# Retention and a gated linear unit on one core: units of 256 tokens with two tokens per partition, and attention products in 64x64 tiles of TensorE

## The chip, the core and the metric

The kernel runs on one core of a Trainium2 chip. The core has TensorE (matmuls, results to PSUM), VectorE, ScalarE and GpSimd (elementwise work), SyncE (here it only issues transfers) and 16 DMA engines. In the profile they are PE (and PEld for its weight loads), DVE, ACT, POOL and SP. The time is the device time of one execution in microseconds; a kernel's time is the median over its runs.

## The reference

There are 8 batches of 576 tokens, 8 heads of width 64. Each head has a decay `gamma = 1 - 2^(-5-h)`. The first part is causal attention without a softmax, weighted by `gamma` to the power of the distance; the second a gated linear unit, whose gate is a causal convolution of five taps per channel:

```python
scores = (1/8) * q @ k.T                               # per batch and head, 576 x 576
ret    = scores * where(i >= j, gamma ** (i - j), 0)
x      = (ret @ v)            # heads side by side: (8, 576, 512)
gate   = sigmoid(sum over t of conv_w[t] * x[:, i - 4 + t, :])
out    = (gate * (x @ w_val)) @ w_out                  # float32, (8, 576, 512)
```

`gamma ** (i - j)` is a product of a factor for `i` and one for `j`. The kernel puts the latter into `v` (tile `gin`) and the former, with the 1/8, onto the result (tile `gout`), so that a mask of ones and zeros is all that a block of scores needs, and what earlier tokens give can be carried in a 64x64 state per head, the sum of `k` times scaled `v`. Inputs and output are float32; the matmuls are bfloat16.

## The kernel before

A chunk is 128 tokens of one batch, one token per partition, all heads. A batch has four full chunks; the last 64 tokens of two batches make a tail chunk. The chunks go through in two groups of four batches, 36 in all. Two neighbouring chunks are a unit of the second part, 256 tokens, 18 in all (a unit of the tails holds 64 tokens of four batches).

For a chunk: `load` issues three transfers on SP's queue, whose runs in memory are one head's row of one token, 256 bytes (L77, L84). `cast` makes bfloat16 copies of k and q and scales v, on GpSimd (L191 to L193). `turn` transposes k and q on TensorE, a pair of heads at a time, into a PSUM tile that VectorE copies for k and ScalarE for q (L205 to L209). `scores` multiplies them in two half-height tiles (64 rows, 128 columns) of TensorE into two PSUM banks (L220); `masks` multiplies each bank by the mask on VectorE (L229). `carried` adds the state's part for a pair of heads with a full 128x128 matmul, the state's off-diagonal blocks being zero (L244, L250). `values` multiplies the masked scores with v in two half-width tiles (L261), and `take_x` scales the result into `xg`, channels on partitions (L270, L274). `update` accumulates the state in a PSUM bank over the chunks of a batch (L289), and ScalarE copies the two diagonal blocks out (L300).

For a unit: `conv` multiplies `xg`, shifted by the tap, with diagonal 64x64 matrices, four tiles of TensorE at once (L322). `gate` is ScalarE's sigmoid (L330). `value` is the product with `w_val` (L337), multiplied by the gate on VectorE (L340); `project` is the product with `w_out` (L347), which ScalarE copies from PSUM (L350) and SP stores, 128 tokens to a transfer (L353, L356).

The order on every engine is written out by hand in the last loop, one slot per chunk (L362 to L401). In slot t the loads of chunk t+6 are issued and chunk t+4 is cast; scores and masks are those of t+1, values and update those of t, transposes those of t+2. A unit's convolution, gate and values stand in the even slots, its projections in the odd ones. PSUM has eight banks: one for transposes, two for scores, one for the attention result, one for the state, three shared by convolution, values and projection.

Of the kernel before, what the change touches and what calls it, by code (L numbers as in the profile page):

```python
# [13 lines left out]
F32 = mybir.dt.float32  # L14
# [7 lines left out]
def kernel(  # L22
# [14 lines left out]
    P = 128  # L37
# [5 lines left out]
    LA = 8  # L43
# [5 lines left out]
    half = ctx.enter_context(tc.tile_pool(name="half", bufs=2))  # L49
    bfp = ctx.enter_context(tc.tile_pool(name="bfp", bufs=4))  # L50
    tp_sb = ctx.enter_context(tc.tile_pool(name="tsb", bufs=3))
    pp = ctx.enter_context(tc.tile_pool(name="pp", bufs=2))
    gp = ctx.enter_context(tc.tile_pool(name="gp", bufs=2))
    op_sb = ctx.enter_context(tc.tile_pool(name="osb", bufs=3))
    xp = ctx.enter_context(tc.tile_pool(name="xp", bufs=1))
    ps_t = ctx.enter_context(tc.tile_pool(name="pst", bufs=1, space=PSUM))
    ps_s = ctx.enter_context(tc.tile_pool(name="pss", bufs=1, space=PSUM))
    ps_o = ctx.enter_context(tc.tile_pool(name="pso", bufs=1, space=PSUM))
    ps_st = ctx.enter_context(tc.tile_pool(name="psst", bufs=1, space=PSUM))
    ps_g = ctx.enter_context(tc.tile_pool(name="psg", bufs=3, space=PSUM))  # L60


    chunks = []
    for g in range(B // GB):
        for b in range(g * GB, (g + 1) * GB):
            chunks += [("full", b, c) for c in range(NCH)]
        chunks += [("tail", b, NCH) for b in range(g * GB, (g + 1) * GB, 2)]
    NT = len(chunks)

    with tc.manual_schedule():  # L70

        loaded = {}

        def load_chunk(b, c):
            for name, src in (("k", k), ("q", q), ("v", v)):
                t = half.tile([P, H, D], F32, name=f"f{name}c", bufs=LA + 1)
                nc.sync.dma_start(out=t, in_=src[b, :, c * P:(c + 1) * P, :].rearrange("h p d -> p h d"))  # L77
                loaded[name, "full", b, c] = t

        def load_tail(b):  # L80
            for name, src in (("k", k), ("q", q), ("v", v)):
                t = half.tile([P, H, D], F32, name=f"f{name}c", bufs=LA + 1)
                for i in range(2):
                    nc.sync.dma_start(out=t[i * TAIL:(i + 1) * TAIL],  # L84
                                      in_=src[b + i, :, NCH * P:S, :].rearrange("h p d -> p h d"))
                loaded[name, "tail", b, NCH] = t

        def load(t):
            kind, b, c = chunks[t]
            if kind == "full":  # L90
                load_chunk(b, c)
            else:
                load_tail(b)

        load(0)
        load(1)

# [4 lines left out]
        nc.scalar.dma_start(out=wvf, in_=moe_w_val.rearrange("(o i) n -> i o n", i=P))  # L102
        load(2)
        wo_src = moe_w_out.rearrange("(pr ab hl p) n -> ab hl p pr n", pr=2, ab=2, hl=2)
        for (p0, blk, ab, hl) in ((0, 0, 0, 0), (64, 0, 1, 0), (0, 2, 1, 1), (64, 2, 0, 1)):
            nc.scalar.dma_start(out=wof[p0:p0 + 64, blk:blk + 2, :], in_=wo_src[ab, hl])
        for t in range(3, LA - 2):
            load(t)
# [7 lines left out]
        nc.vector.tensor_copy(identf, ident[0:32, 0:32])  # L116

        mask = consts.tile([P, P], BF16, name="mask")
        nc.gpsimd.memset(mask, 1.0)
        nc.gpsimd.affine_select(mask, mask, pattern=[[1, P]], base=0, channel_multiplier=-1,  # L120
                                compare_op=ALU.is_ge, fill=0.0)
        mask_t = consts.tile([P, P], BF16, name="maskt")
        nc.vector.tensor_copy(mask_t, mask)
        nc.vector.memset(mask_t[0:64, 64:128], 0.0)

        lrow = consts.tile([P, H], F32, name="lrow")
        lcol = consts.tile([P, NP], F32, name="lcol")
        for h in range(H):
            nc.vector.memset(lrow[:, h:h + 1], -lng[h])
            nc.vector.memset(lcol[(h % 2) * 64:(h % 2) * 64 + 64, h // 2:h // 2 + 1], lng[h])  # L130
        toki = consts.tile([P, NCH + 1], mybir.dt.int32, name="toki")
        nc.gpsimd.iota(toki, pattern=[[P, NCH + 1]], base=0, channel_multiplier=1)
        tok = consts.tile([P, NCH + 1], F32, name="tok")
        nc.vector.tensor_copy(tok, toki)
        nc.vector.tensor_scalar(tok[64:128, NCH:NCH + 1], tok[64:128, NCH:NCH + 1], -64.0, None, op0=ALU.add)
        gin = consts.tile([P, NCH + 1, H], F32, name="gin")
        nc.vector.tensor_tensor(gin, tok.unsqueeze(2).to_broadcast([P, NCH + 1, H]),
                                lrow.unsqueeze(1).to_broadcast([P, NCH + 1, H]), op=ALU.mult)
        nc.scalar.activation(gin, gin, AF.Exp)

        posi = consts.tile([P, S], mybir.dt.int32, name="posi")
        nc.gpsimd.iota(posi, pattern=[[1, S]], base=0, channel_multiplier=0)
# [7 lines left out]
        sbd = [consts.tile([P, NP, P], BF16, name=f"sbd{i}") for i in range(2)]  # L150
        sbl = [consts.tile([P, NP, P], BF16, name=f"sbl{i}") for i in range(GB)]
        for t in sbd + sbl:
            nc.gpsimd.memset(t, 0.0)
# [8 lines left out]
        def prep_conv():  # L162
            cps = ps_t.tile([P, KC * NP], F32, name="tps")
# [10 lines left out]
        def prep_wv():  # L174

            src = wvf.rearrange("p o (pr ab hl j) -> p o pr ab hl j", pr=2, ab=2, hl=2)
            for (blk, j0, ab, hl) in ((0, 0, 0, 0), (0, 64, 1, 0), (2, 0, 1, 1), (2, 64, 0, 1)):
                nc.scalar.copy(wvb[:, :, blk:blk + 2, j0:j0 + 64], src[:, :, :, ab, hl, :])
# [3 lines left out]


        bf = {}

        def cast(t):
            kind, b, c = chunks[t]
            kb = bfp.tile([P, H, D], BF16, name="kb")
            qb = bfp.tile([P, H, D], BF16, name="qb")
            vb = bfp.tile([P, H, D], BF16, name="vb")  # L190
            nc.gpsimd.tensor_copy(kb, loaded["k", kind, b, c])  # L191
            nc.gpsimd.tensor_copy(qb, loaded["q", kind, b, c])  # L192
            nc.gpsimd.tensor_tensor(vb, loaded["v", kind, b, c],  # L193
                                    gin[:, c, :].unsqueeze(2).to_broadcast([P, H, D]), op=ALU.mult)
            bf[t] = (kb, qb, vb)

        tsb = {}

        def turn(t):
            kb, qb, vb = bf[t]  # L200
            ps = ps_t.tile([P, 2, NP, P], BF16, name="tps")
            for i, src in enumerate((kb, qb)):
                flat = src.rearrange("p h d -> p (h d)")
                for pr in range(NP):
                    nc.tensor.transpose(ps[:, i, pr, :], flat[:, pr * P:(pr + 1) * P], ident)  # L205
            kt = tp_sb.tile([P, NP, P], BF16, name="kt")
            qt = tp_sb.tile([P, NP, P], BF16, name="qt")
            nc.vector.tensor_copy(kt, ps[:, 0])  # L208
            nc.scalar.copy(qt, ps[:, 1])  # L209
            tsb[t] = (kt, qt)  # L210

        sps = {}

        def scores(t):
            kt, qt = tsb[t]
            s = [ps_s.tile([P, NP, P], F32, name=f"s{i}") for i in range(2)]
            for pr in range(NP):
                for i in range(2):
                    r = slice(i * 64, i * 64 + 64)
                    nc.tensor.matmul(s[i][:, pr, :], lhsT=kt[r, pr, :], rhs=qt[r, pr, :],  # L220
                                     start=(pr == 0), stop=(pr == NP - 1), skip_group_check=True)
            sps[t] = s

        pt = {}

        def masks(t, i):
            m = mask if chunks[t][0] == "full" else mask_t
            p = pp.tile([P, NP, P], BF16, name=f"p{i}")
            nc.vector.tensor_tensor(p, sps[t][i], m.unsqueeze(1).to_broadcast([P, NP, P]), op=ALU.mult)  # L229
            pt[t, i] = p  # L230

        ops = {}
        state = {}

        def carried(t):

            kind, b, c = chunks[t]
            o = ps_o.tile([P, NP, P], F32, name="o")
            ops[t] = o
            qt = tsb[t][1]  # L240
            if kind == "full":
                if c:
                    for pr in range(NP):
                        nc.tensor.matmul(o[:, pr, :], lhsT=state[b][:, pr, :], rhs=qt[:, pr, :],  # L244
                                         start=(pr == 0), stop=False, skip_group_check=True)
            else:
                for pr in range(NP):
                    for i in range(2):
                        cs = slice(i * TAIL, (i + 1) * TAIL)
                        nc.tensor.matmul(o[:, pr, cs], lhsT=state[b + i][:, pr, :], rhs=qt[:, pr, cs],  # L250
                                         start=(pr == 0 and i == 0), stop=False, skip_group_check=True)

        def values(t):
# [25 lines left out]
        def update(t):  # L279
# [4 lines left out]
            if c == 0:  # L284
                st[b] = ps_st.tile([P, NP, P], F32, name="st")
# [145 lines left out]
```

## Time and profile before

| what | value |
|---|---|
| median of 3 runs | 195.38 us (195.11 to 197.34) |
| span of the profiled execution, first to last instruction | 194.1 us |
| median less the profiled span | 1.3 us |
| granted TensorE clock, mean over the span | 0.986 of full speed |
| TensorE matmul busy, weight loads | 152.2 us in 2273, 111.0 us in 2273 |
| VectorE, ScalarE, GpSimd busy | 114.3, 89.3, 86.9 us |
| moved by DMA | 40.21 MB in 118919 packets, 113242 of them under 512 bytes |
| SP's queue (inputs and outputs) | 117760 packets, 37.76 MB, 86.3% of 16 engines' time |
| inputs, 256 KB each: issue to landing | 4.8 to 5.3 us |
| outputs, 256 KB each: issue to landing | 3.8 us |

An execution's own time is given for the timed runs alone; for the profiled one the page has its span, and sums are made against that. Busy time is the union of an engine's instructions. A matmul's duration there is its latency, so the rate of a series is read from its starts. The slices are fortieths of the span, 4.85 us each, with busy shares in tenths. The chain of waits goes back from the last instruction, at each step to what released it. A line of the groups has the source line, engine, operation, output and inputs, shapes and count, then busy time, mean duration in ns, and the idle time before these instructions with what ended it.

### The profile page before, as it was taken

To read this page: it belongs to the slowest core of one execution; us is meant where nothing else is said; L and a number is where in the kernel's file an instruction comes from. 1 tells how busy PE (TensorE), PEld (TensorE's weight loads), DVE (VectorE), ACT (ScalarE), POOL (GpSimd) and SP (SyncE) were. 2 spreads that over 40 slices of the span, in tenths; PEclk is the share of its full clock that TensorE was granted. 3 is DMA by queue.
4 is the path that set the end of the run, shared out by engine and by line. 5 is a ranking of instruction groups with operands and counts; after the bars stand their busy time and mean duration, and the time that the engine had idled before them with its cause. 6 is when DMAs were issued, how large, how long until landed. Compare 5 with 4: busy or idle time off the path is not lost.

```text
span 194.1 us, 5639 instructions
## 1 busy us (share of the span) xinstructions
PE 152.2 (78%) x2273; PEld 111.0 (57%) x2273; DVE 114.3 (59%) x211; ACT 89.3 (46%) x183; POOL 86.9 (45%) x126
## 2 busy tenths in 40 slices
PE   0112666998898989898988899788989898979990
PEld 0001545775666676667766576666666666667740
DVE  6406774747475657575766657474766575747420
ACT  0072635354646454444435464446463535354431
POOL 8214685655454626453644534454445362520000
PEclk9999999699999999999999999999999999999997
DMA  5999999999999999799999795999997998931124
GB/s 136 287 205 163 220 223 182 234 221 200 256 250 238 247 230 255 158 243 216 277 193 281 169 282 127 231 231 280 233 237 187 245 253 187 237 142 62 52 105 108
DMA packets 118919, 40.21 MB, mean 207 GB/s; under 512 B 113242, under 2 KB 113262, under 8 KB 118894
## 3 DMA queue, kind: packets, MB, share of 16 engines
q1 hardware_dynamic: 117760, 37.76, 86.3%
q10 hardware_dynamic: 1134, 2.11, 4.2%
q8 instruction: 17, 0.28, 0.7%
q14 instruction: 8, 0.07, 0.1%
HBM read 30.42 MB, written 9.44 MB: 205 GB/s over the span
## 4 chain that ended last, share of the span: by engine, by line
PE 48%; DMA 18%; ACT 12%; DVE 9%; SPq 4%; issue 4%; POOL 1%; ACTq 0%; DVEq 0%; POOLq 0%
PE g L337 10%; PE g L347 9%; PE g L322 9%; DMA fvc<-in_v_dram 7%; ACT qt L209 6%; DMA out_dram<-ob 5%; DMA fkc<-in_k_dram 5%; PE tps L205 5%; PE s L220 5%; PE o L261 4%; ACT gate L330 4%; PE st L289 4%; DVE kt L208 4%; DVE p L229 3%; SPq L77 2%
## 5 line engine op out<-in xcount | busy, mean ns | idle before, releaser
L229 DVE TENSOR_TENSOR p<-s,mask 128x512 bf16<-128x512 f32 x64 | 43.7, 684 | 19.3 <-PE s L220 19.3
L337 PE MATMUL g<-xg,wvb 128*128 128x256 bf16 x288 | 37.1, 272 | 14.7 <-ACT gate L330 13.4
L193 POOL TENSOR_TENSOR vb<-fvc,gin 128x512 bf16<-128x512 f32 x36 | 37.5, 1043 | 22.2 <-DMA fvc<-in_v_dram 16.0
L340 DVE TENSOR_TENSOR z<-gate,g 128x512 bf16<-128x512 f32 x36 | 24.8, 688 | 33.4 <-ACT gate L330 24.7
L337 PEld LDWEIGHTS <-wvb 128*128 128x128 bf16 x288 | 27.3, 97 | 21.1 <-issue 18.3
L191 POOL CAST kb<-fkc 128x512 bf16<-128x512 f32 x36 | 22.9, 636 | 31.9 <-DMA fkc<-in_k_dram 21.1
L192 POOL CAST qb<-fqc 128x512 bf16<-128x512 f32 x36 | 22.2, 617 | 29.4 <-DMA fqc<-in_q_dram 29.2
L347 PE MATMUL g<-wob,z 128*128 128x512 bf16 x144 | 34.4, 380 | 0.3 <-DVE z L340 0.3
L209 ACT COPY qt<-tps 128x512 bf16<-128x512 bf16 x36 | 21.1, 585 | 26.8 <-DVE kt L208 25.6
L350 ACT COPY ob<-g 128x512 f32<-128x512 f32 x36 | 21.0, 589 | 19.7 <-DMA out_dram<-ob 14.1
L300 ACT CAST sbd<-st 64x256 bf16<-64x256 f32 x48 | 17.6, 367 | 25.2 <-PE st L289 24.7
L322 PE MATMUL g<-xg,dg 64*64 64x256 bf16 x720 | 23.2, 271 | 0.0
L208 DVE COPY kt<-tps 128x512 bf16<-128x512 bf16 x36 | 15.1, 421 | 11.8 <-PE tps L205 11.7
L270 DVE TENSOR_TENSOR xg<-o,gout 128x512 bf16<-128x512 f32 x32 | 21.8, 681 | 0.0
L347 PEld LDWEIGHTS <-z 128*128 128x128 bf16 x144 | 13.3, 99 | 13.7 <-DVE z L340 1.2
L205 PE MATMUL tps<-ident,kb 128*128 128x128 bf16 x144 | 14.9, 229 | 7.1 <-POOL kb L191 7.1
L330 ACT ACTIVATE gate<-g 128x512 f32<-128x512 f32 x36 | 19.6, 601 | 1.7 <-PE g L322 1.7
L322 PEld LDWEIGHTS <-dg 64*64 64x64 bf16 x720 | 18.4, 106 | 2.0 <-issue 0.4
L205 PE MATMUL tps<-ident,qb 128*128 128x128 bf16 x144 | 14.9, 229 | 5.7 <-POOL qb L192 5.7
L220 PE MATMUL s<-qt,kt 64*128 64x128 bf16 x288 | 15.0, 225 | 4.5 <-ACT qt L209 4.3
L220 PEld LDWEIGHTS <-kt 64*128 64x128 bf16 x288 | 10.1, 96 | 10.2 <-DVE kt L208 4.1
L261 PE MATMUL o<-p,vb 128*64 128x128 bf16 x288 | 15.4, 230 | 0.0
(45 smaller groups left out, 108.1 us busy)
## 6 DMA issues: line engine op xcount, KB each, us to landing
fkc<-in_k_dram SPq DMA_DIRECT2D x32, 256.0 KB, 5.0
fqc<-in_q_dram SPq DMA_DIRECT2D x32, 256.0 KB, 5.3
fvc<-in_v_dram SPq DMA_DIRECT2D x32, 256.0 KB, 4.8
out_dram<-ob SPq DMA_DIRECT2D x32, 256.0 KB, 3.8
wvf<-in_moe_w_val_dram ACTq DMA_DIRECT2D x1, 1024.0 KB, 9.7
wof<-in_moe_w_out_dram ACTq DMA_DIRECT2D x4, 256.0 KB, 10.5
fkc<-in_k_dram SPq DMA_DIRECT2D x8, 128.0 KB, 3.4
fqc<-in_q_dram SPq DMA_DIRECT2D x8, 128.0 KB, 3.3
```

Source lines behind the costliest of these rows:

```text
L191: nc.gpsimd.tensor_copy(kb, loaded["k", kind, b, c])
L193: nc.gpsimd.tensor_tensor(vb, loaded["v", kind, b, c], gin[:, c, :].unsqueeze(2).to_broadcast([P, H, D]), op=ALU.mult)
L205: nc.tensor.transpose(ps[:, i, pr, :], flat[:, pr * P:(pr + 1) * P], ident)
L209: nc.scalar.copy(qt, ps[:, 1])
L220: nc.tensor.matmul(s[i][:, pr, :], lhsT=kt[r, pr, :], rhs=qt[r, pr, :], start=(pr == 0), stop=(pr == NP - 1), skip_group_check=True)
L229: nc.vector.tensor_tensor(p, sps[t][i], m.unsqueeze(1).to_broadcast([P, NP, P]), op=ALU.mult)
L261: nc.tensor.matmul(o[r, pr, :], lhsT=vb[:, 2 * pr + i, :], rhs=pt[t, i][:, pr, :], start=(fresh and pr == 0), stop=(pr == NP - 1), skip_gr ...
L322: nc.tensor.matmul(g[bank][cols, pr, :], lhsT=dg[rows, blk, kk, :], rhs=xs(n, rows, blk, kk), start=(pr == 0 and kk == 0), stop=(pr == 1 a ...
L330: nc.scalar.activation(t, gps[n][i], AF.Sigmoid)
L337: nc.tensor.matmul(vps[:, j, :], lhsT=wvb[:, o, 2 * i + j, :], rhs=xs(n, slice(0, P), o, PAD), start=(j == 0 and o == 0), stop=(j == 1 and ...
L340: nc.vector.tensor_tensor(z, gsb[n][i], vps, op=ALU.mult)
L347: nc.tensor.matmul(o, lhsT=zsb[n, j // 2][:, j % 2, i * P:(i + 1) * P], rhs=wob[:, j, :], start=(j == 0), stop=(j == NP - 1))
```

## The change

The kernel is rewritten around units of 256 tokens; both parts go unit by unit.

- A partition holds two neighbouring tokens, so a run of the inputs is 512 bytes and of the output 4 KB. A tail unit has four batches' last 64 tokens, 32 partitions each. Loads are issued four units ahead, and a unit's output is one tile and one transfer (four for a tail), issued in the next unit's step behind that step's loads.
- The two tokens of a partition are index `r`. Tokens stand in PSUM in the order (r, a), token 2a + r of 128; masks and `gout` follow it, and `take_x` writes them back in order.
- All attention products are 64x64 tiles of TensorE, issued in rounds of four (`QUAD`), one for each quarter of the array: transposes (64 a unit), scores (32), masked products (32), update (32). The carried state uses the two tiles that lie on one diagonal and then those on the other.
- Masks and the PSUM copies of transposes take two banks in one instruction. ScalarE now copies k and q; the state is summed on GpSimd from a float32 copy that ScalarE makes.
- PSUM: two banks shared by transposes and convolution, two by scores and update, two for the attention result, two for values and projections. All four of the first kinds have a single buffer.
- The value and output weights are loaded on SP's queue between inputs. Eight products of zeros are issued at the start. In the first unit GpSimd casts units 0 and 1 before the first state sums, k of unit 0 is cast on VectorE, and two small copies (`fence`) part the first carried products.

```diff
-        def load_chunk(b, c):
...
+        def load1(n, u):
+            t = ldp.tile([P, H, 2 * D], F32, name=f"f{n}c")
+            if kind == "full":
+                nc.sync.dma_start(out=t, in_=src[b, :, c * W:(c + 1) * W, :].rearrange("h (p r) d -> p h (r d)", r=2))
...
-        nc.scalar.dma_start(out=wvf, in_=moe_w_val.rearrange("(o i) n -> i o n", i=P))
-        load(2)
+        nc.sync.dma_start(out=wvf, in_=moe_w_val.rearrange("(o i) n -> i o n", i=P))
+        load(1)
...
+    QUAD = ((0, 0), (1, 1), (0, 1), (1, 0))
...
+        def turn(u):
+            ps = ps_a.tile([P, 2, 2, 2, 2, 2, 64], BF16, name="a")
+            for hf in range(2):
+                for i in range(2):
+                    for prl in range(2):
+                        for r in range(2):
+                            for (c, par) in QUAD:
+                                h = 2 * (2 * hf + prl) + par
+                                nc.tensor.transpose(ps[half[par], c, hf, i, prl, r, :], bf[u][i][half[c], h, r, :],
+                                                    ident[half[c], half[c]])
...
+        def take_turn(u, hf):
+            nc.scalar.copy(kqt[u][hf].rearrange("p c i l r a -> p c (i l r a)"),
+                           tps[u][:, :, hf].rearrange("p c i l r a -> p c (i l r a)"))
...
+        def scores(u, hf, between=None):
+            s = ps_s.tile([P, 2, 2, 2, P], F32, name="s")
+            t = kqt[u][hf]
+            for prl in range(2):
+                for r in range(2):
+                    for (c, par) in QUAD:
+                        nc.tensor.matmul(s[half[c], par, prl, r, :], lhsT=t[half[par], c, 0, prl, r, :],
+                                         rhs=t[half[par], c, 1, prl, :, :].rearrange("p r a -> p (r a)"),
+                                         start=True, stop=True, skip_group_check=True)
+                    if between and prl == 0 and r == 0:
+                        between()
...
+        def masks(u, hf):
+            nc.vector.tensor_tensor(p.rearrange("p e l r a -> p (e l) (r a)"),
+                                    sps[u, hf].rearrange("p e l r a -> p (e l) (r a)"),
+                                    m.rearrange("p r a -> p (r a)").unsqueeze(1).to_broadcast([P, 4, W]), op=ALU.mult)
...
+        def carried(u, odd):
+            for pr in range(NP):
+                t = kqt[u][pr // 2]
+                for c in range(2):
+                    par = c ^ odd
+                    rows = half[par]
...
+                        nc.tensor.matmul(o[rows, c, pr, :], lhsT=st[rows, pr, :],
+                                         rhs=t[rows, c, 1, pr % 2, :, :].rearrange("p r a -> p (r a)"),
...
+        def values(u, hf):
+            for prl in range(2):
+                for r in range(2):
+                    for (c, par) in QUAD:
+                        nc.tensor.matmul(o[half[par], c, pr, :], lhsT=vb[half[c], 2 * pr + par, r, :],
+                                         rhs=p[half[c], par, prl, r, :], start=first(u, c, par),
...
+        def update(u):
+            xy = ps_s.tile([P, 2, 512], F32, name="s")
+            for pr in range(NP):
+                for r in range(2):
+                    for (c, par) in QUAD:
+                        nc.tensor.matmul(xy[half[par], c, pr * 64:pr * 64 + 64], lhsT=kb[half[c], h, r, :],
+                                         rhs=vb[half[c], h, r, :], start=(pr == 0 and r == 0), stop=(pr == NP - 1 and r == 1),
...
+            xf = stp.tile([P, 2, NP, 64], F32, name="xf")
+            nc.scalar.copy(xf.rearrange("p c o d -> p c (o d)"), xy[:, :, 0:NP * 64])
...
+                nc.gpsimd.tensor_tensor(mid, state[b, "run"], xf[:, 0], op=ALU.add)
+                nc.gpsimd.tensor_copy(s1, mid)
+                s2 = stp.tile([P, NP, 64], BF16, name=f"s4{b % GB}", bufs=1)
+                nc.gpsimd.tensor_tensor(s2, mid, xf[:, 1], op=ALU.add)
...
+        for n in range(NU):
+            if ok(n + 4):
+                load(n + 4)
+            if n >= 1:
+                store(n - 1)
+            conv(n)
+            if n == 0:
+                turn(n + 1)
+                take_turn(n + 1, 0)
+                take_turn(n + 1, 1)
+                update(n + 1)
+            else:
+                if_ok(carried, n + 1, 0)
+                if_ok(scores, n + 1, 0)
+                if_ok(masks, n + 1, 0)
+            value(n, 0)
+            gated(n, 0)
+            value(n, 1)
...
+            if ok(n + 1):
+                scores(n + 1, 1, lambda: carried(n + 1, 1))
+                masks(n + 1, 1)
+            gated(n, 1)
+            if n == 0:
+                prep_wo()
+            if ok(n + 2):
+                turn(n + 2)
+                take_turn(n + 2, 0)
+                take_turn(n + 2, 1)
+            if_ok(values, n + 1, 1)
+            if_ok(values, n + 1, 0)
+            if_ok(take_x, n + 1)
+            if_ok(update, n + 2)
+            project(n, 0)
+            project(n, 1)
+            if_ok(cast, n + 3)
```

## The prediction

> **What bounds the kernel now.** I read the page's slices first (who is busy when), then the chain of waits in order of time (what a unit's period is made of), then the groups (what one instruction costs). Two rows of the slices matter: TensorE and the DMA engines.
>
> ```profile
> span 194.1 us, 5639 instructions
> ...
> PE 152.2 (78%) x2273; PEld 111.0 (57%) x2273; DVE 114.3 (59%) x211; ACT 89.3 (46%) x183; POOL 86.9 (45%) x126
> ...
> PE   0112666998898989898988899788989898979990
> DMA  5999999999999999799999795999997998931124
> ```
>
> The DMA row is full until about 172 us, when the last inputs are in; TensorE reaches its level only at about 29 us. Yet the steady middle is not paced by arrivals. The chain of waits, from one convolution to the next:
>
> ```profile
> 49.98 1.22 PE g L322 x40
> 51.53 0.46 PE tps L205 x8
> 52.02 0.44 DVE kt L208
> 52.48 0.59 ACT qt L209
> 53.06 0.51 ACT gate L330
> 53.61 1.05 PE g L337 x8
> 54.81 0.54 issue
> 55.36 0.68 DVE p L229
> ...
> 58.30 0.40 PE s L220 x8
> 58.69 0.34 PE o L261 x8
> 59.04 1.22 PE g L322 x40
> ```
>
> A unit (256 tokens) takes 59.04 - 49.98 = 9.06 us, and the chain holds no DMA there: it hops from TensorE to copy, gate and mask and back. The convolutions start every 9.05 us, except for a second one at 40.9, four long periods (9.98, 9.33, 9.47 and the first) and a last of 5.5; the last starts at 183.6. So the span is 40.9 us to the second convolution, 142.7 us for the next 16, and 10.5 us behind the last. In 9.05 us the unit moves 2.1 MB (1.57 in, 0.52 out), 232 GB/s: the DMA engines are nearly, not quite, the bound too.
>
> ```profile
> L229 DVE TENSOR_TENSOR p<-s,mask 128x512 bf16<-128x512 f32 x64 | 43.7, 684 | 19.3 <-PE s L220 19.3
> L337 PE MATMUL g<-xg,wvb 128*128 128x256 bf16 x288 | 37.1, 272 | 14.7 <-ACT gate L330 13.4
> L322 PE MATMUL g<-xg,dg 64*64 64x256 bf16 x720 | 23.2, 271 | 0.0
> ```
>
> The mean of 271 ns is one matmul's latency. The rate is in the timeline: 40 matmuls of 64x64, 256 columns, start over 1.12 us, four in each 112 ns; the full-array ones of 256 columns start every 108.5 ns. So four-way packing works in this kernel already and costs 3 ns per round.
>
> **Loads and stores.** Each partition takes two neighbouring tokens, so 110,592 input packets of 256 bytes become 55,296 of 512, and 4,608 output packets of 2 KB become 2,304 of 4 KB. Packet records of the trace: 256 bytes take 18 ns (median; mean 20), the 20 packets of 512 bytes (convolution weights) 27, the 2 KB ones 84 (mean 100). By a line through 256 bytes and 2 KB, 4 KB is 159. Before: (110,592 x 20 + 5,632 x 100)/16 = 173 us of every engine, which is the full row. After, with means 1.12 to 1.19 over medians: (55,296 x 30 + 2,304 x 185 + 1,024 x 100)/16 = 137 us, 7.6 us a unit. Bounds: if a 512-byte packet is worth two of 256 (40 ns) it is 171 us, no gain; at the medians 123. On SP the store of a unit now stands behind the next unit's three loads and waits for the second output copy; nothing but loads four units ahead is queued behind it, and with two output buffers the next writer comes a whole period later, against 3.8 us to landing now. SP issues four transfers a unit in place of eight, at 0.4 to 2 us each, so it is relieved. The weights' loads move from ScalarE's queue to SP's: ScalarE, whose first table load waited until 10.96 us behind 9.00 us of issuing the output weights, is free to form the decay factors by about 7 us, and SP has five more transfers to pass before unit 1's and 2's inputs.
>
> [...]
>
> **TensorE.** Per unit, before to after: transposes 16 of 128x128 to 64 of 64x64 (64 columns); scores 16 to 32; products with the mask 16 to 32; state update 8 to 32 (64 columns); carried state 8 to 8 or 16 (two tiles at once). Convolution (1.12), value (16 x 108.5 ns = 1.74) and projection (8 x 216 = 1.73) stay. From the starts: 128-column matmuls go at 55 ns each on the full array and 55 to 56 a pair in half tiles, so before, the attention products need (16 + 8 + 8 + 8 + 8) x 55 = 2.6 us. After they are 16 + 8 + 8 + 8 rounds of four and 4 steps or more of carried state. The price of a round is the disputed cost: no row has rounds of 64 or 128 columns. From below, streaming: 58 ns at 128 columns (55 + 3) and about 31 at 64 (a second 64-column weight load starts 27 to 29 ns after the first), 2.0 us in all. From above, the highest sustained instruction rate on record, the convolution's 8 instructions (4 loads, 4 matmuls) per 112 ns, 14 ns each: 172 pairs x 28 = 4.8 us. Bursts are much denser: the first 8 instructions of a convolution start within 28 ns, often 12. I take 56 ns for every round, 7 ns an instruction, twice that burst's 3.5 and half the sustained 14: 2.5 us.
>
> [...]
>
> Changes of tile shape cost TensorE about 90 ns (last half-tile start to first convolution start 147 against 56); there are about eight a unit before, four after.
>
> **The other engines, per unit.** A two-bank operation doubles the elements: VectorE's 256 elements take 415 ns and 512 take 684, so 1,024 are 1.22 us. Masks 2 x 1.22, gating 2 x 0.69, x 2 x 0.68 = 5.2 us, and the key copies (2 x 0.42) go to ScalarE. ScalarE: sigmoid 1.07, two copies of 1.05, state 0.59, outputs 2 x 0.59 = 4.9. GpSimd: casts 2 x (0.64 + 0.62 + 1.04) = 4.6, and new state sums on 256 elements, three, each under a cast's 0.64: 1.3 to 1.9. All are under 8 us and hidden, if their order lets them.
>
> **The period.** TensorE's order from convolution n at 0, in us: convolution to 1.12, carried and first scores (0.44) to 1.56, change and both values to 3.39, change, second scores with carried between to 3.93, transposes of n+2 (0.9) to 4.83. VectorE: first mask 1.8 (result latency 0.2) to 3.02, first gate 3.71, second mask 4.13 to 5.35, second gate 6.04. TensorE waits for that mask at 4.83, does the masked products 5.4 to 5.85 and the update to 6.3, change, projects 6.4 to 8.1, change: 8.2. The x multiplications (6.04 to 7.4) and the copies of the transposes are done before the next convolution. The new wait is scores on one buffer of two banks: the second half queues behind the first mask, covered by the 1.74 us of values (without them it would cost 1.2). Behind the wait for the second mask stand update, projection and the next convolution. State goes PSUM, ScalarE, GpSimd, TensorE: copy ends by 7.7, sums by 8.9, wanted at 9.3: 0.4 us of cover. I take 8.3.
>
> **Start and end.** On the SP queue stand inputs 0, value weights, inputs 1, output weights, inputs 2 and 3. The third tensor of unit 1 ends 4.19 MB: about 15 us of packets after 2 us. GpSimd casts unit 1 (last cast ends near 19) before it forms the first state, which the carried products wait for; then products, x, convolution 0 near 23. Unit 1 goes through gate 25.7, transposes and copies 29, state 30.6, scores, masks, gate 34.8, the weights' cast (1.33, on VectorE) and x: second convolution near 38, against 40.9. The tail stays at 10.5: fewer packets, but the last store waits for both halves.
>
> **Sum.** 38.1 + 16 x 8.3 = 132.8, less 1.3 (the last two periods lack update and transposes), + 10.5 = 180.1; half of the present long periods' excess (1.6), 0.8: span 180.9. The median lies 1.3 above the profiled span: **182 us**. Own range of this case 176 to 188.
>
> **Rivals.**
> - *Instruction supply binds TensorE.* Above some rate the small tiles no longer overlap. Then the period is the plain sum 1.12 + 1.74 + 1.73 + 0.36 + 172 x pair. At 14 ns an instruction it is 9.8 us: 38.1 + 1.5 (transposes in the start) + 156.8 - 2.7 + 10.5 + 1.3 = 205.5, slower. It decides from 24.7 ns a pair (period 9.2), where the gain is gone. For it: nothing in the trace sustains less than 12.5 ns. Against: bursts, and every such row is explained by streaming alone. Chance of over 199: 0.21.
> - *Partly so, or bytes bind.* At 10 ns an instruction the period is 8.7: 187. If 512-byte packets bring nothing, 171 us of DMA after 2 of start and 20 behind the last input (22 now) leave 193. These and their mixtures, 188 to 199: 0.24, of which 0.07 is below 191.5.
> - *Better than thought.* A period of 8.0 with a second convolution at 34 (GpSimd's first casts not in the way): 34 + 128 - 1.3 + 9.5 + 1.3 = 171.5. Below 176: 0.13.
>
> The forecast has 0.42. A measurement of this kernel tells about 2% from no change (191.5 to 199.3). Faster 0.42 + 0.13 + 0.07 = 0.62, same 0.17, slower 0.21. The range, 172 to 202, leaves out the ends of the first and third rival.
>
> **What will show it.** Convolution starts 8.3 us apart; DMA row under nine tenths in the middle; 64 transposes started in 0.9 us (0.5 if streaming alone, 1.8 if supply binds: the row to look at first); TensorE waiting for the second mask, not for GpSimd's state; second convolution near 38 us. I am wrong if the transposes are slow, if the state sums come late, or if SP's issue falls behind (12 loads for each tail unit, at about 0.5 us each).

## The result and the profile after

| | before | changed |
|---|---|---|
| median | 195.25 us (194.55 to 197.34) | 202.88 us (201.89 to 204.96) |
| ratio | | 1.038 [1.032, 1.045]: slower |
| profiled span, granted clock | 194.1 us, 0.986 | 200.8 us, 0.914 |
| second convolution starts | 40.9 us | 39.74 us |
| the next 16 periods | 142.8 us | 150.45 us |
| behind the last convolution's start | 10.5 us | 10.6 us |

Ratios, here and below, are to the kernel before in the same session and leave out executions over 1.5% above the fastest of their kernel, which the medians and ranges of times include.

The forecast was 182 us, in a range of 172 to 202. Start and end came out near it; the 16 periods hold the error, 150.45 us against 132.3.

The page of the changed kernel; the row `q8 instruction` (packets, MB, share of 16 engines' time) is one that the prediction did not look at:

```profile
span 200.8 us, 9197 instructions
...
PE 152.2 (76%) x4233; PEld 108.2 (54%) x4233; DVE 98.2 (49%) x147; ACT 90.2 (45%) x117; POOL 99.2 (49%) x119
...
PE   6324595885978989698929978769788969889790
...
PEclk9955559699999999879995899999999999999999
DMA  5999999986688789929590957891967702022023
...
q8 instruction: 33, 0.54, 1.1%
...
L253 DVE TENSOR_TENSOR p<-s,mask 128x1024 bf16<-128x1024 f32 x32 | 39.2, 1225 | 66.1 <-PE s L243 66.1
```

The same row of the kernel before:

```profile
q8 instruction: 17, 0.28, 0.7%
```

The DMA row left its ceiling, as forecast. But TensorE's row has slices of 2, 6 and 7 in the middle, and its granted clock, once at 9, falls to 8, 7 and 5 again. Matmuls went from 2273 to 4233. A matmul and its weight load are two instructions: 4546 before, 8466 after. The instruction queue moved 17 and then 33 packets of 16 KB, about one for each 256 of these (4546/256 = 17.8, 8466/256 = 33.1).

The chain of waits in order of time (start, duration, what; both in us), first an undisturbed unit, then a disturbed one:

```profile
50.62 1.22 PE a L380 x40
...
52.29 1.85 PE v L394 x16
...
54.76 1.24 DVE p L253
56.00 0.04 issue
56.04 0.63 PE o L304 x30
56.67 0.26 PE s L337 x28
56.93 1.83 PE v L406 x8
58.77 0.34 PE a L380 x5
59.10 0.63 issue
...
100.09 1.24 DVE p L253
101.33 0.04 issue
101.37 0.63 PE o L304 x30
102.00 0.23 PE s L337 x24
102.23 3.24 issue
105.47 0.31 PE s L337 x5
105.78 3.53 PE v L406 x8
```

The first unit is the forecast almost to the tenth: convolution, values, wait for the second mask, masked products, update, projection, and the next convolution 8.15 us after the last. In the second unit TensorE stops in the middle of the 32 products of the update. `issue` means that it waits for nothing that the profile shows: no semaphore, no operand. After 3.24 us it goes on with the same series, and the projection behind it takes 3.53 us in place of 1.83, at a granted clock of 0.50 (mean of 105.4 to 109.2 us), the 5 of the row above.

There are twelve such stops of more than 0.6 us between two starts, 18.06 us together, and none in the steady middle of the kernel before. If TensorE's instructions are numbered in order of start (from 0; matmuls, weight loads and the 22 records of its sequencer), every one stands just ahead of number 256 j + 193, j a whole number. That is the grid of the instruction queue's packets. Four of its blocks, in us, from the packet records:

| block begins on TensorE | packet of the next block starts | takes | lands | next block wanted | got | pause |
|---|---|---|---|---|---|---|
| 59.73 | 62.57 | 0.92 | 63.49 | 63.91 | 64.83 | 0.93 |
| 99.70 | 103.19 | 0.92 | 104.12 | 102.03 | 105.47 | 3.43 |
| 160.38 | 161.56 | 1.22 | 162.78 | 162.77 | 164.11 | 1.35 |
| 164.11 | 165.33 | 0.91 | 166.24 | 170.14 | 170.14 | none |

With one exception among 33 (a block whose first instruction still waited for data) the packet of the next 256 instructions starts only after the present 256 have begun: 0.4 to 1.2 us after it in the nine blocks with almost no data beside it (at most two data packets in flight as the block begins and again halfway to the packet's start), in the median 2.9 us (1.0 to 4.0) in the 15 where a dozen or more are in flight as the block begins. It takes 0.9 to 1.8 us, mostly about 1, and where a pause shows, TensorE goes on 1.27 to 1.60 us after it lands. The block that begins at 164.11 lasts 6.03 us, its packet is in after 2.13, and no pause follows. The undisturbed unit's last line is already the next stop, 0.90 us from start to start. A unit has 464 to 480 of them in 8.15 us, 4.4 us a block on average, but the block from the second scores to the middle of the update lasts only 2.3 us (99.70 to 102.03), one with projection and convolution 6 (164.11 to 170.14).

After three of the stops, at 36.35, 84.19 and 105.78 us, the projection ran at half clock, 3.4 to 3.5 us for 1.83, and once the convolution behind it (2.3 us for 1.22); the granted clock is 0.57, 0.60 and 0.50 in the mean of 36.0 to 39.8, 83.5 to 87.7 and 105.4 to 109.2 us, and 0.57 from 109.2 to 112. Behind the second convolution that is 1.63 + 1.70 + 1.06 = 4.4 us. Pauses there are 16.9 us. At 8.15 us, and 7.9 for the last two, 16 undisturbed periods make 129.9; the excess of 20.5 us is those 21.3, less what fell into the wait for a mask that was due anyway.

### The profile page after: what moved, and what is told of

Its sections match the earlier page's. It is cut to its first block, busy times and chain, and to the rows that moved or that the text cites. A ratio compares the mean times of both kernels' runs of the same rounds, so it can differ in the third digit from the quotient of the medians.

```text
span 200.8 us, 9197 instructions
## 1 busy us (share of the span) xinstructions
PE 152.2 (76%) x4233; PEld 108.2 (54%) x4233; DVE 98.2 (49%) x147; ACT 90.2 (45%) x117; POOL 99.2 (49%) x119
## 3 DMA queue, kind: packets, MB, share of 16 engines
q1 hardware_dynamic: 60240, 39.85, 66.9%
## 4 chain that ended last, share of the span: by engine, by line
PE 69%; DVE 11%; issue 9%; DMA 4%; SPq 3%; POOL 1%; ACT 1%; DVEq 0%
PE v L406 19%; PE v L394 17%; PE a L380 13%; DVE p L253 10%; PE s L243 6%; PE o L304 6%; DMA fvc<-in_v_dram 4%; PE o L281 3%; PE s L337 3%; SPq L86 2%; PE a L225 1%; POOL vb L208 1%; SPq L102 1%; DVE xg L315 1%; ACT gate L384 1%
## 5 line engine op out<-in xcount | busy, mean ns | idle before, releaser
L253 DVE TENSOR_TENSOR p<-s,mask 128x1024 bf16<-128x1024 f32 x32 | 39.2, 1225 | 66.1 <-PE s L243 66.1
L231 ACT COPY kq<-a 128x1024 bf16<-128x1024 bf16 x36 | 34.7, 1015 | 49.4 <-PE a L225 49.4
L406 PE MATMUL v<-wob,z 128*128 128x512 bf16 x144 | 39.3, 421 | 0.2
L394 PE MATMUL v<-xg,wvb 128*128 128x256 bf16 x288 | 36.1, 279 | 0.7 <-issue 0.7
L208 POOL TENSOR_TENSOR vb<-fvc,gin 128x1024 bf16<-128x1024 f32 x18 | 34.7, 1926 | 1.4 <-DMA fvc<-in_v_dram 1.4
L410 ACT COPY ob<-v 128x512 f32<-128x512 f32 x36 | 21.0, 591 | 20.0 <-PE v L406 20.0
L380 PE MATMUL a<-xg,dg 64*64 64x256 bf16 x720 | 26.4, 288 | 4.3 <-issue 2.7
L399 DVE TENSOR_TENSOR z<-gate,v 128x512 bf16<-128x512 f32 x36 | 24.4, 679 | 10.4 <-PE v L394 7.6
L384 ACT ACTIVATE gate<-a 128x1024 f32<-128x1024 f32 x18 | 18.4, 1024 | 20.9 <-PE a L380 19.9
L243 PE MATMUL s<-kq 64*64 64x128 bf16 x576 | 21.6, 228 | 4.1 <-DVE p L253 2.7
L207 POOL CAST qb<-fqc 128x1024 bf16<-128x1024 f32 x18 | 19.8, 1100 | 3.2 <-DMA fqc<-in_q_dram 3.2
L243 PEld LDWEIGHTS <-kq 64*64 64x64 bf16 x576 | 14.9, 107 | 8.0 <-issue 6.3
```

The costliest lines, as they stand in the source:

```text
L208: nc.gpsimd.tensor_tensor(vb.rearrange("p h r d -> p (h r) d"), loaded["v", u].rearrange("p h (r d) -> p (h r) d", r=2), gin[:, c].rearran ...
L231: nc.scalar.copy(kqt[u][hf].rearrange("p c i l r a -> p c (i l r a)"), tps[u][:, :, hf].rearrange("p c i l r a -> p c (i l r a)"))
L243: nc.tensor.matmul(s[half[c], par, prl, r, :], lhsT=t[half[par], c, 0, prl, r, :], rhs=t[half[par], c, 1, prl, :, :].rearrange("p r a -> p ...
L253: nc.vector.tensor_tensor(p.rearrange("p e l r a -> p (e l) (r a)"), sps[u, hf].rearrange("p e l r a -> p (e l) (r a)"), m.rearrange("p r ...
L380: nc.tensor.matmul(g[cols, bank, pr, :], lhsT=dg[rows, blk, kk, :], rhs=xs(u, rows, blk, kk), start=(pr == 0 and kk == 0), stop=(pr == 1 a ...
L384: nc.scalar.activation(t, g, AF.Sigmoid)
```

## Experiments

The theory: TensorE's instructions arrive in blocks of 256, and a block takes longer than the changed kernel needs to run through one. The rivals: small tiles don't overlap (the prediction's rival), a wait for data or for VectorE that the trace doesn't name, the new order with its single buffers, or a clock that drops of itself.

**What a block costs, alone.** Two kernels run only 512 rounds of four 64x64 tiles on constants, 4096 instructions without a wait, once with nothing beside and once beside the input loads of all full units. A store to the output follows.

```diff
+        for i in range(512):
+            for (c, par) in QUAD:
+                nc.tensor.matmul(s[half[par], c, 0:64], lhsT=a[half[c], 0:64], rhs=a[half[c], 64:128], ...)
+        if LOADS:   # the second kernel: the inputs of all full units
+            nc.sync.dma_start(out=t, in_=src[b, :, c * W:(c + 1) * W, :].rearrange("h (p r) d -> p h (r d)", r=2))
```

> Nothing of the computation is done: TensorE runs 512 rounds of four 64x64 matmuls of 64 columns on constants, 4096 instructions with the weight loads, no transfers beside it. If the pauses of the changed kernel come from fetching TensorE's instructions in blocks of 256 (theory A), the stream pauses every 256 instructions and takes 3.4 to 4 us a block (1.2 us to the block's packet, 1.0 for it, 1.35 until its first instruction starts), 55 to 64 us in all. If TensorE's own issue sets the pace (rival B), the starts are even, without pauses. If neither binds, 512 rounds of 30 ns are 15 us.

> The same stream of 4096 TensorE instructions, with 24 MB of the inputs loaded beside it in packets of 512 bytes that nothing reads. Theory A: a block waits for its packet behind the data, as in the changed kernel (2.5 to 3.7 us to its start), so 5 to 6 us a block while loads run, 80 to 96 us in all. Rival B: as without the loads, since no instruction waits for data.

The timeline of TensorE without loads (start, duration, merged instructions, idle time before and what ended it):

```profile
9.47 1.93 PE L58 MATMUL s<-a 64*64 64x64 bf16 x128 [1.53 <-issue]
13.20 1.92 PE L58 MATMUL s<-a 64*64 64x64 bf16 x128 [1.80 <-issue]
16.92 1.92 PE L58 MATMUL s<-a 64*64 64x64 bf16 x128 [1.80 <-issue]
```

And beside the loads:

```profile
13.86 1.92 PE L58 MATMUL s<-a 64*64 64x64 bf16 x128 [3.45 <-issue]
18.68 1.93 PE L58 MATMUL s<-a 64*64 64x64 bf16 x128 [2.90 <-issue]
24.88 1.92 PE L58 MATMUL s<-a 64*64 64x64 bf16 x128 [4.27 <-issue]
```

The series comes in pieces of exactly 128 matmuls (256 instructions) that take 1.92 us, and then nothing. The tiles overlap, four in 53 ns; in the 1.5 to 4.3 us between the pieces above, TensorE waits for nothing that the profile shows. Fourteen blocks took 53.3 us without loads, **3.81 us a block**, and 73.3 us beside them, **5.24 us**: 14.9 and 20.5 ns an instruction. The streams end at 60.0 and 82.4 us, in the ranges expected; with the store the kernels took 112.16 and 138.93 us, one execution each. This settles the cost and that transfers raise it. The granted clock of the second kernel is recorded as 0.50; the profile of the first holds no record of it, so its mean of 1.00 tells nothing. Within a piece both start a round of four every 53 ns. That is the rate of the same form in the changed kernel where the clock is recorded as 0.50 (the 64 transposes at 25.53 us); at full clock it is 33 to 36 ns in the median of a series that no stop cuts. So as far as the rate tells, both streams ran at half clock, and the pair differs in the transfers alone.

**The transfers taken away.** In the changed kernel only k is loaded, and q and v are read from its tile; instructions and order on TensorE stay.

```diff
-            for n in "kqv":
-                load1(n, u)
+            load1("k", u)
+            loaded["q", u] = loaded["v", u] = loaded["k", u]
```

> The changed kernel with k loaded alone; q and v are taken from the same tile, so two thirds of the input bytes are left out and the values are others. Every TensorE instruction stays. Theory A: the packets of instructions start after about 1.2 us, the pauses without a wait sum to under 6 us in place of 19.7, convolutions come 8.1 to 8.5 us apart, 176 to 185 us. Rival B (TensorE's work or issue): the same pauses, over 195 us.

```profile
span 186.2 us, 9098 instructions
...
PE   5134676896989898898959898979798898989780
...
DMA  5999000043152442716240717434361211203024
```

It took 187.88 us, in one execution. TensorE's no-wait gaps over 0.2 us at block boundaries sum to 5.3 us in place of 19.7: 14.4 us less, nearly all of the 14.6 that the span lost (200.8 to 186.2). Three stops over 0.6 us are left. The time lies 2.9 us above the range that I expected: the 16 periods are 8.6 us in the mean, not 8.1 to 8.5, two of them 10.8 and 11.2 with a stop and half clock behind it. That the pauses grow with the transfers is thus seen in the kernel itself, at the same mean clock (0.917 against 0.914).

**Fewer instructions, same work.** The transposes go back to the full array: k and q lie in SBUF as [P, 2, H, D], a pair of heads is a 128x128 transpose, and 64 small ones become 16. In a second kernel the update, too, takes half-height products for pairs of heads, 16 for 32.

```diff
-                            for (c, par) in QUAD:
-                                h = 2 * (2 * hf + prl) + par
-                                nc.tensor.transpose(ps[half[par], c, hf, i, prl, r, :], bf[u][i][half[c], h, r, :],
-                                                    ident[half[c], half[c]])
+                            h = 2 * (2 * hf + prl)
+                            nc.tensor.transpose(ps[:, hf, i, prl, r, :],
+                                                bf[u][i][:, r, h:h + 2, :].rearrange("p h d -> p (h d)"), ident)
...
-                    for (c, par) in QUAD:          # update, second kernel only
-                        nc.tensor.matmul(xy[half[par], c, pr * 64:pr * 64 + 64], lhsT=kb[half[c], h, r, :], ...)
+                    for c in range(2):
+                        nc.tensor.matmul(xy[:, c, pr * P:pr * P + P]..., lhsT=kb[half[c], r, hs, :]..., ...)
```

> The changed kernel with the transposes alone on the full array: 368 to 376 TensorE instructions a unit (before 256, changed 464 to 480, with the update too 336 to 344). Theory A: a unit of about 8.3 us fetches 1.45 blocks, 5.7 us each, about what a busy fetch needs: pauses sum to 1 to 6 us, 185 to 191 us. If the update's shape and not the count mattered: near 202 us.

> The changed kernel with transposes on the full array (16 a unit in place of 64) and the update in half-height tiles (16 in place of 32): 336 to 344 TensorE instructions a unit in place of 464 to 480, but 0.6 us more of streaming and two more changes of tile shape; k and q are written by GpSimd in another order. Theory A: a block lasts a unit's three quarters, about 6 us, most fetches are hidden, the pauses without a wait sum to under 8 us: 182 to 190 us. Rival B: TensorE's longer work shows, 16 x 0.6 = 10 us, over 205 us.

The kernel with full-array transposes alone, its page:

```profile
span 180.0 us, 7469 instructions
...
PE 151.2 (84%) x3369; PEld 112.8 (63%) x3369; DVE 98.4 (55%) x147; ACT 88.9 (49%) x117; POOL 99.1 (55%) x119
...
PE   5253578589999999998999999999999999998880
...
q8 instruction: 26, 0.43, 1.0%
```

It took 183.19 us (181.62 to 183.70), 0.938 [0.932, 0.944] of the kernel before and a little under the range expected; with the update changed as well 186.11 us, 0.946 [0.941, 0.952]. The 864 matmuls less are 1728 instructions less, and seven packets less. One stop of 0.70 us is left in the first, none in the second, and the rest of the kernel is the change's own: masks, pairs of tokens, packed scores. The first kernel's periods are 8.145 us, the same as an undisturbed unit of the change, although the full-array transposes stream longer (1.00 us for the 16 in a chain of waits shown below, 0.65 us for the 64 small ones of the changed kernel): there is room for them in the wait for the second mask. In the second kernel the period is 8.45 us. Its update, behind that mask, takes 0.55 us in the chain of waits in place of the 0.26 above, which is nearly the whole difference; ScalarE's copies of the state, now in two pieces, are not in that chain:

```profile
63.27 0.55 PE s L335 x16
```

Once the stops are gone, fewer instructions bring nothing more.

**Instructions put into the kernel before.** Thirteen rounds of four small products a chunk raise it to 464 instructions a unit; a control adds about as much streaming in four wide products a unit.

```diff
+            for _ in range(13):
+                for (a, e) in ((0, 0), (1, 1), (0, 1), (1, 0)):
+                    nc.tensor.matmul(s[a][hv[e], 0, 0:64], lhsT=kt[hv[a], 0, 0:64], rhs=kt[hv[a], 0, 64:128], ...)
...
+            for _ in range(2):     # the control
+                nc.tensor.matmul(s[0]...[:, 0:448], lhsT=kt[:, 0, :], rhs=kt...[:, 0:448], ...)
```

> The kernel before, with 13 rounds of four 64x64 matmuls of 64 columns ahead of each chunk's scores; what they write is overwritten. TensorE has 464 instructions a unit, as the changed kernel, and 0.8 us a unit more of streaming. Theory A (instructions are fetched in blocks of 256): 1.8 blocks a unit at 5 to 6 us, 9.1 to 10.9 us a unit; pauses without a wait at every 256th instruction or so, over 8 us in sum; 203 to 228 us. Rival C (the pauses belong to the new order and its single buffers, not to the number of instructions): no such pauses, 196 to 208 us.

> The kernel before, with the same streaming time (0.75 us a unit) in four full-array matmuls a unit of 448 columns. 264 instructions a unit. Theory A and rival C: no pauses without a wait; 196 to 208 us, and by theory A at least 5 us less than with the small tiles.

209.47 us, 1.072 [1.063, 1.080], and 201.92 us, 1.033 [1.023, 1.043]. The difference of 7.5 us has the size that I expected, but the trace doesn't bear the reason out: there is one stop over 0.6 us (1.07), not many. The rounds lie on this kernel's chain, 0.54 us a chunk where the control's products take 0.38:

```profile
77.23 0.54 PE s L220 x52
```

```profile
74.97 0.38 PE s L218 x2
```

Over 36 chunks that is 5.8 of the 7.0 us between the two profiled spans. The rounds lengthen the unit to 9.93 us, so that a block lasts 9.93 x 256/464 = 5.48 us, just above the 5.24 that it costs. The test **can't tell the theories apart**; it only agrees with the price of a block.

**Instructions put back where there is room.** The better test adds them to the kernel with full-array transposes, ahead of `turn`, in front of the wait for the mask: 12 rounds of four small transposes of the identity (464 instructions a unit again) against seven full-array ones of about the same streaming time (382).

```diff
+            for _ in range(12):
+                for (c, par) in QUAD:
+                    nc.tensor.transpose(ps[half[par], c, 0, 0, 0, 0:64], ident[half[c], half[c]], ident[half[c], half[c]])
...
+            for _ in range(7):     # the control
+                nc.tensor.transpose(ps[:, 0, 0, 0, 0, :], ident, ident)
```

> The version with transposes on the full array, and ahead of them 12 rounds of four 64x64 transposes of the identity into the same banks, which the real ones overwrite: 464 TensorE instructions a unit again, and 0.37 us of streaming, which falls into TensorE's wait for the second mask (about 1 us). The stream of constants cost 5.24 us a block of 256 beside loads and 3.81 without. Theory A: 1.81 blocks in 8.15 us leave 4.5 us a block, so pauses of 0.7 us a block and more return at every 256th instruction, over 8 us in sum: 193 to 204 us. Rival C (order and single buffers make the pauses): none, 183 to 185.

> The same with seven full-array transposes in their place: 0.39 us of streaming, 382 instructions a unit. Theory A: 5.5 us a block, pauses under 3 us in sum, 183 to 187 us. If the streaming itself cost the time: as much as with the small ones.

The page with the small ones, and a piece of its chain of waits:

```profile
span 200.4 us, 9197 instructions
...
PE   6434586894989999996949979869999989999790
...
q8 instruction: 33, 0.54, 1.1%
```

```profile
44.27 1.00 PE a L227 x16
45.27 0.57 PE o L305 x32
45.84 0.24 PE s L338 x30
46.09 2.56 issue
48.65 0.22 PE s L338 x2
```

The page with the full ones:

```profile
span 180.8 us, 7721 instructions
...
PE   5443579789999999999999999999899999998880
...
q8 instruction: 27, 0.44, 1.0%
```

201.68 us (198.39 to 203.93), 1.030 [1.012, 1.048], against 184.29 us (182.40 to 185.38), 0.943 [0.936, 0.952]. The holes in TensorE's row are back with 33 packets, eleven stops of 16.7 us together, all ahead of number 256 j + 193, four of them in the middle of an update as in the change; with 27 packets there is one (0.89). Tiles of the real work, changes of tile shape, order, buffers, masks and transfers are the same in both. The added transposes start over 0.52 us a unit in the first and 0.35 in the second, in front of the wait for the mask: periods without a stop are 8.16 and 8.15 us. Nor does the clock, as far as it is recorded, explain it. The profiled execution of the first took 202.03 us at a recorded clock of 0.925, but two others took 198.39 and 201.33 us at 0.995 and 0.989, while the control took 182.40 and 183.41 at 0.943 and 0.931. That is the theory shown: in this pair the loss follows the count of instructions (464 and 382 a unit), whatever they compute.

**The start.** Two more edits, for the 39 us to the second convolution. One leaves the eight products of zeros out and casts k of unit 0 ahead of the convolution's preparation (on the kernel with transposes and update changed). The other moves the transposes and the update of unit 1, and the cast of the output weights, into the first unit's own part, where engines wait for inputs (on the kernel with transposes changed).

```diff
-        warm(8)
-        prep_conv()
-        cast(0, nc.vector)
+        cast(0, nc.vector)
+        prep_conv()
```

> The full-array version without the eight products of zeros at the start, and with k of unit 0 cast on VectorE ahead of the convolution's preparation. In the full-array version the chain at the start goes through the zeros (1.9 to 5.5 us) and the preparation (to 7.6) to that cast. If this chain sets the start: the first transposes begin 2 to 4 us earlier and the time falls by 1 to 3 us, to 183 to 185. If arrivals and GpSimd's casts of unit 1 set it, as the prediction had it: no change, 185.5 to 187.

```diff
         update(0)
+        turn(1)
+        take_turn(1, 0)
+        take_turn(1, 1)
         carried(0, 0)
...
         take_x(0)
+        update(1)
         prep_wv()
+        prep_wo()
...
-            if n == 0:
-                turn(n + 1)
-                take_turn(n + 1, 0)
-                take_turn(n + 1, 1)
-                update(n + 1)
-            else:
-                if_ok(carried, n + 1, 0)
-                if_ok(scores, n + 1, 0)
-                if_ok(masks, n + 1, 0)
+            if_ok(carried, n + 1, 0)
+            if_ok(scores, n + 1, 0)
+            if_ok(masks, n + 1, 0)
...
```

> The version with transposes on the full array, with the transposes and the update of unit 1 ahead of convolution 0 and its state sums so earlier, and the cast of the output weights there too. In the first unit transposes, copies, state and scores of unit 1 now stand one behind another between the first and the second convolution (22 to 38.5 us). If that chain sets the start: second convolution 4 to 8 us earlier, 175 to 179 us. If arrivals set it: under 2 us, 181 to 183.

Without the products of zeros: 185.33 us, 0.948 [0.944, 0.953], no different from 0.946 with them; the second convolution moved from 40.25 to 39.40 us only. With unit 1's work moved ahead:

```profile
span 173.4 us, 7469 instructions
...
PE   5355879999999999999999999999999999996970
...
DMA  4999999999999999999789769999787020303114
```

**175.84 us** (175.08 to 179.13), 0.905 [0.900, 0.910], the fastest kernel of this study. The second convolution starts at 32.62 us in place of 38.49, the periods stay at 8.145, and TensorE's row is full from 26 us on. So in that version the order of the work, and not arrivals, bound the start.

## Why the prediction was wrong, step by step

- **The period without pauses**: worked out as 8.2, taken as 8.3, measured 8.15 (50.55 to 58.70 in the chain). The chain named is the one that ends last, the wait for the second mask is where it was put, and GpSimd's state is not waited for behind the start (there once, 2.0 us).
- **Loads and stores**: right. Median 27 ns for packets of 512 bytes and 159 for 4 KB, as taken; SP's queue 66.9% of 200.8 us, 134 us, for 137.
- **Operations over two banks**: masks 1225 ns (1.22 forecast), copies of transposes 1015 (1.05), sigmoid 1024 (1.07). GpSimd's casts 1.04, 1.10 and 1.93 us for 1.27, 1.24 and 2.09.
- **The price of a round**, called the disputed cost: I took 56 ns. The 64 transposes start over 0.65 us where no stop cuts them (0.9 forecast, 1.8 if supply bound), 41 ns a round, and 80 instructions in a row start within 360 ns, 4.6 ns apart. That nothing sustains less than 12.5 ns holds for the trace of before alone. My price was too high, and most of it hid behind the mask, so it cost the forecast little.
- **The step that failed** is the period of 8.3 us, which holds no term for the delivery of instructions. What stood for it was the bound *from above*, "the highest sustained instruction rate on record", 14 ns each from the convolution's series. Such a series of 80 instructions is shorter than a block of 256, so its rate says what TensorE can run through, not what reaches it. The sum needed a second bound, on 256 instructions at once: 5.24 us beside loads, 20.5 ns an instruction or 41 a pair. The runs showed in its place 16.9 us of stops in the 16 periods, and 4.4 us of half clock behind two of them. The fastest block of the kernel before lasts 8.84 us (86.13 to 94.97), 35 ns an instruction, and I asked for 17 (8.15 us for 470) without a row for it.
- **The rival "Instruction supply binds TensorE"** had the right word and the right sign, at 0.21, but not this mechanism: it let tiles stop overlapping, with a plain sum of 9.8 us in every period. Measured are periods of 7.9 and 8.15 us between others of up to 13.4, 9.40 on average. The trace that it demanded, slow transposes, did not come (three of the 18 series hold a stop, the other 15 take 0.59 to 0.83 us); by that view it would have been called refuted, while supply did bind. Its 205.5 us lies near the 202.88 by luck.
- **The start**: 38.1 forecast, 39.74 measured, of it 1.19 us of a pause and 1.57 of half clock behind it. Half clock is recorded from 9.21 to 29.69 us too, with the first convolution at 2.35 us (1.3 later) and the first values at 3.23 (1.9), which the forecast didn't have. So the rest was shorter than forecast, and the nearness is in part luck. **The end**: 10.5 forecast, 10.6 measured.
- **In sum**: 1.6 (start) + 18.1 (periods) + 0.1 (end) on the forecast span of 180.9 give 200.8.

The trace of before held the warning. There the packet of the next block lands 1.8 to 3.8 us after a block has begun, and 5 to 8 us before it is wanted (once 9.7), because a block lasts about a whole unit, 9.05 us. The change puts nearly two blocks in a shorter unit, 4.4 us each. Landing at up to 3.8 us leaves almost none of that; what stayed unknown was the 1.27 to 1.60 us that TensorE takes after a landing, for which before has no row.

## What to carry to other kernels

Count an engine's instructions for each stage and set them against the stage's time: here 256 TensorE instructions (128 matmuls with their weight loads) took 5.24 us in the stream beside loads and 3.81 us in the one without, and the change to smaller tiles raised the count from 256 a unit to between 464 and 480 for the same work. The sign here was a stop marked `issue` inside a series that has no wait, at a spacing of 256 instructions (twelve over 0.6 us, 18.06 us together), with 33 packets of the instruction queue beside 17 before. The remedy was not to give the packing up but to keep it where it shortens the chain and take full-array forms where there is room: 16 transposes for 64 turned 202.88 us (1.038 of the kernel before) into 183.19 (0.938), and work moved into the idle start brought 175.84 (0.905).

## What the runs showed of the hardware

- Instructions are not free of the transfers: in the changed kernel a packet of them starts 0.4 to 1.2 us after its block has begun with almost no data in flight, 2.9 us in the median beside a dozen data packets or more, and in the two streams a block took 3.81 us without loads and 5.24 us beside them. The packets have 16 KB, and all twelve stops over 0.6 us stand just ahead of an instruction numbered 256 j + 193. TensorE started 80 instructions at 4.6 ns each and stood still for 18.06 us of one execution.
- Four tiles of the array together started a round of four 64-column transposes, with four weight loads, every 41 ns over 64 transposes (0.65 us where no stop cuts them, in the changed kernel); where the clock is recorded as 0.50 the median is 53 ns.
- A pause can cost twice. After three of the twelve stops, of 1.19, 1.33 and 3.43 us, the clock is recorded as 0.50 for 3.41, 3.41 and 6.83 us; after a stop of 2.57 us it is not (the projection behind it took 1.83 us), nor after a second one of 1.19 us (118.78 to 119.97). The clock records of the changed kernel, all but the last, span whole multiples of 3.41 us (3.41 to 88.75), and in the 3.41 us just before each of these three half clocks TensorE was busy for 1.63, 1.51 and 0.85 us. The stop of 2.57 us falls on two such stretches, busy for 2.06 and 1.60 us. So the length of the stop alone does not decide, and busy time doesn't part 1.60 from 1.63; what does is not shown, as no run moved a stop.
